# Clustered attention and token mixing on one core: a slot list for each half of the array's rows

## The chip, the cores and the metric

The kernel runs on one core of a Trainium2 chip. The metric is the device time of one execution in microseconds (us); lower is better. Five engines work side by side on a core: TensorE (PE, with its weight loads PEld), VectorE (DVE), ScalarE (ACT), GpSimd (POOL) and SyncE (SP), whose queue issues nearly all DMAs here. Each engine has a queue of its own, and in the profile an instruction that waits holds up what stands behind it on its engine.

## The reference

```python
# q, k, v: 4 batches x 8 heads x 768 x 64; centroids: 8 x 16 x 64
q_assign = np.argmax(np.einsum('bhsd,hcd->bhsc', q_n, c_n), axis=-1)    # normalised q, centroids
k_assign = np.argmax(np.einsum('bhsd,hcd->bhsc', k_n, c_n), axis=-1)
mask = q_assign[:, :, :, None] == k_assign[:, :, None, :]
scores = np.where(mask, scale * np.matmul(q, k.transpose(0, 1, 3, 2)), -1000000000.0)
attn = np.exp(scores - np.max(scores, axis=-1, keepdims=True))
attn = attn / (np.sum(attn, axis=-1, keepdims=True) + 1e-09)
x = (attn @ v), heads side by side                                       # 4 x 768 x 512
theta = x @ w_theta
y = w_tok_r @ (x * cos(theta)) + w_tok_i @ (x * sin(theta))              # over the 768 tokens
u = x + y
out = u + np.maximum(u @ w_ch, 0.0)
```

## The kernel before

**Stages.** Attention comes first (about 25 to 437 us of the profiled execution), token mixing second (from there to the end); the first rotation of the second stage is already computed while attention ends.

**Attention.** Two heads form a *pair* (16 pairs, `pi`). The two heads lie in the two halves of the 128 partitions, `j` = 0 in rows 0 to 63 and `j` = 1 in rows 64 to 127, so a matmul of one head uses half of the array's rows, and two matmuls with different `j` run side by side. Here such a place for one matmul of each half is called a **slot**. A *unit* is one tile of 128 keys for one half of the queries (12 units to a pair, 192 in all). For each unit and head the scores take four matmuls into one PSUM bank (`score_products`, tile `sc`), an exponential on ACT (`exps`, L437, tile `at`), a running sum over three tiles on POOL (`add_exps`, L448, tile `acc`), and two matmuls of the weighted sum (`weighted`, L509, tile `av`). The row maxima that the scores need are computed ten units ahead: four matmuls per head into two banks (`max_products`, tile `m`), reduced by one DVE instruction (`max_of`, L396).

**A block.** The main loop (L702) takes two units, `u` and `u + 1`, in a pass, which is called a **block** here; six blocks make a pair. A block has 12 slots and eight matmuls of weighted sums, in this order: four slots with both heads of unit `u` (`both`), four with head 0 of `u + 1` beside the maxima of one head of unit `u + 10` (`scores_beside_max`), the weighted sums of the two units before, and four slots with head 1 of `u + 1` beside the maxima of the other head. Blocks are named below by their first unit within the pair: 0, 2, 4, 6, 8, 10.

**Banks.** PSUM has eight: four for two `m` tiles, one for `av`, three that rotate (`bank`, L199), used for the scores and for all small results (`lg`, `lt`, `mt`, `rt`, `sm`). A rotating pool hands out the bank that was handed out longest ago, and the first matmul into it waits until its last reader is done.

**Pieces.** Everything else in attention is cut into small pieces that are given out by a table of due units: `pieces(u)` runs those due up to `u`, ahead of the weighted sums, behind them, and at the end of the block. On PE: `mt` (the transposed maxima, L404), `lg` and `lt` (the cluster products and their transposes, L263, L275), `sm` (sums, L476). On DVE: the argmax over 16 clusters, which reads `lt` in PSUM (L278 the maximum, L280 where it is reached, L284 and L286 its index), `mk` (L339), `add_sums` (L452), and the unpacking of weights (L137, L140, L143, L146). On POOL: the low parts `lq`, `lk` (L360), `xt` times `rb` (L530), the low parts of weights (L159). On ACT: copies out of PSUM, the high parts (L356), the mask's `Abs` and `Relu` (L335, L337). Within attention the code's order is the order on every engine (`in_order`). After it, the framework's scheduler orders the instructions.

**The end of attention.** `first_rotation` (L550) loads 128 tokens twice: `xs` for the angle `theta` (L608), and `xb`, four DMAs (L596) that DVE turns into token-major `xn` (L601). There is one `xb` buffer, so the DMAs of the next block wait for the turn before. DVE reduces the angle with L613, L614, L615; the bank of the next angle's matmuls is free once L614 has read it.

Of the kernel before, what the change touches and what calls it, by code (L numbers as in the profile page):

```python
# [9 lines left out]
F32 = mybir.dt.float32  # L10
# [6 lines left out]
PSUM = bass.MemoryType.PSUM  # L17

BIG = float(2.0 ** 60)
N_M = 2  # L20
N_AV = 1
# [20 lines left out]
def kernel(  # L42
# [136 lines left out]
    actx = ExitStack()  # L179

    ps0 = actx.enter_context(tc.tile_pool(name="ps0", bufs=N_M, space=PSUM))
    ps = actx.enter_context(tc.tile_pool(name="ps", bufs=8 - 2 * N_M - N_AV, space=PSUM))
# [13 lines left out]
    def m_tile(name):  # L196
        return ps0.tile([P, 2, 512], F32, tag="m", name=name)

    def bank(name):  # L199
        return ps.tile([P, 512], F32, tag="bank", name=name)  # L200
# [47 lines left out]
    def assign(pi):  # L248
# [172 lines left out]
    def score_products(u, j, banks=None):  # L421
# [5 lines left out]
        sc = banks[:, j] if banks else ps.tile([P, 512], F32, tag="bank", name=f"sc{u}_{j}")  # L427
# [28 lines left out]
        for j in range(2):  # L456
            then(u, j)

    def scores_beside_max(u, v, j):

        interleave(score_products(u, j), max_products(v, 1 - j))
        exps(u, j)
        max_of(v, 1 - j)

    def sums(pi):

# [47 lines left out]
                s["xt"] = p2.tile([P, 2, HS], F32, tag="xt", name=f"xt{pi}", bufs=3)  # L514

    def weighted_out(u):
        pi, a, i = split_u(u)
        s = st[pi]
        if i == NT - 1:

            if u == NUT - 1:
# [28 lines left out]
    def first_rotation():  # L550

        xs = ma[0].tile([P, NCT, P], F32, tag="ab", name="xs")
        nc.sync.dma_start(out=xs, in_=xT_d[0][:, :, 0:P])
        yield
        load_blocks(0)
# [4 lines left out]
        rotation_turn(0, xn)  # L560
        yield
        rotation_angle(xh, xl, tp)
        yield
        ab = rotation_reduce(0, "0_0", tp, kk, r)
        first.update(r=r, ab=ab, xn=xn)

    first = {}
# [134 lines left out]
    while u <= NUT or todo:  # L702
        start = len(nc.cur_bb.bb.instructions)
        ahead = u + LEAD

        def pieces(u):
            for x in sorted(x for x in todo if x <= u):
                for fn, a in todo.pop(x):
                    fn(*a)

        if 0 <= u < NUT:
            both(score_products, u, exps)
            add_exps(u)
            if ahead < NUT:
                scores_beside_max(u + 1, ahead, 0)
# [12 lines left out]
        if 0 <= u < NUT:  # L728
            if ahead < NUT:
                scores_beside_max(u + 1, ahead, 1)  # L730
            else:

                both(score_products, u + 1, exps, *([m_tile(f"sc{u + 1}")] if u < NUT - 6 else []))
            add_exps(u + 1)
        if 0 < u and ahead < NUT:
            weighted_out(u - 1)
        pieces(u + 1)
        in_order(start)
        u += 2
# [64 lines left out]
    def theta(b, t):  # L804
        n, name = b * NT + t, f"{b}_{t}"
        xs = xts[b][:, :, t * P:(t + 1) * P]
        xh, xl, xn, kk, r = rotation_tiles(n, name)

        late = n == AHEAD
        rotation_parts(xs, xh, xl, last_out[0] if late else None)  # L810
        rotation_turn(n, xn)
        tp = mbank(f"tp{name}")
        with behind(last_rows[0] if late else None):
            rotation_angle(xh, xl, tp)
        ab = rotation_reduce(n, name, tp, kk, r)
        rotate(b, t, r, ab, xn)

    def rotate(b, t, r, ab, xn):
# [188 lines left out]
```

## Time and profile before

| | |
|---|---|
| times of three runs | 795.07, 795.83, 797.3 us (median 795.83) |
| profiled execution | 797.01 us, of which the profile's span is 795.2 us |
| PE, DVE, ACT, POOL busy | 97%, 72%, 49%, 61% of the span |
| attention's steady part | 60 to 420 us of the span |
| one block without pieces on PE | 3.88 us |
| one pair (six blocks with their pieces) | 25.95 us |

The page gives shares over the whole span; attention and token mixing have quite different limits, so the views by stretches of time, and the timeline of single engines, tell more. In a timeline row the first number is the start in us from the span's start, the second the time until the group's last instruction ended, then engine, line, operation, what it writes and reads, and the count; the bracket holds idle time of the engine ahead of it and what ended it. A matmul of 384 columns stands with 0.33 to 0.34 us though the next begins 0.17 us behind it: ends overlap, so starts are compared.

### The profile page before, as it was taken

The numbers are of one execution on the slowest core, as the hardware profiler recorded it, in microseconds if no ns is written. First come the engines' busy times: TensorE is split into PE (matmuls) and PEld (weight loads), VectorE is DVE, ScalarE is ACT, GpSimd is POOL, SyncE is SP. The second block draws the span as 40 slices with busy tenths as digits, with TensorE's granted clock in tenths as the row PEclk, the third lists the DMA queues.
The fourth block names the chain that finished last, engine by engine and source line by source line (L and its number), as shares of the span: only waits on it lengthen the run. The fifth ranks groups of instructions, "written<-read, shape, count | busy, mean of one in ns | idle before, by whom it ended". The sixth has DMA issues, their size and how long they took to land.

```text
span 795.2 us, 14306 instructions
## 1 busy us (share of the span) xinstructions
PE 774.7 (97%) x5538; PEld 574.3 (72%) x5538; DVE 573.3 (72%) x688; ACT 386.9 (49%) x777; POOL 488.4 (61%) x284
## 2 busy tenths in 40 slices
PE   7999999999999999999999599999999999999998
PEld 5665656565665666666665378899888988899998
DVE  5889999999999999999889368954435343634322
ACT  3466666666767676666655335451324123403310
POOL 3479888999999999888988141571125122332131
PEclk9999999999999999999999899999999999999999
DMA  3233314342443234433352267024111411030001
GB/s 120 61 96 97 110 55 148 124 115 73 143 132 112 85 127 152 131 108 125 123 187 69 68 177 237 17 41 166 20 27 28 158 28 27 14 93 14 1 21 61
DMA packets 81584, 73.45 MB, mean 92 GB/s; under 512 B 59588, under 2 KB 65324, under 8 KB 81132
## 3 DMA queue, kind: packets, MB, share of 16 engines
q1 hardware_dynamic: 81228, 72.10, 30.5%
q8 instruction: 44, 0.72, 0.4%
q10 hardware_dynamic: 288, 0.43, 0.1%
q14 instruction: 24, 0.20, 0.1%
HBM read 57.08 MB, written 15.32 MB: 91 GB/s over the span
## 4 chain that ended last, share of the span: by engine, by line
PE 92%; DVE 5%; DMA 1%; SPq 1%; issue 1%; ACT 1%; DVEq 0%; ACTq 0%
PE y L876 26%; PE sc L374 25%; PE av L509 16%; PE tp L608 8%; PE cy L899 5%; PE m L374 3%; PE cp L899 3%; PE sm L476 2%; PE lg L263 1%; PE y L899 1%; DVE nm L396 1%; PE lt L275 1%; PE mt L404 1%; DVE acc L452 1%; SPq L596 1%
## 5 line engine op out<-in xcount | busy, mean ns | idle before, releaser
L437 ACT ACTIVATE at<-sc 128x384 f32<-128x384 f32 x384 | 173.6, 494 | 96.7 <-PE m L374 57.7
L396 DVE TENSOR_REDUCE nm<-m 128x1 f32<-128x768 f32 x192 | 179.7, 945 | 19.6 <-PE m L374 16.6
L448 POOL TENSOR_TENSOR acc<-at,at 128x768 f32<-128x768 f32 x64 | 130.4, 2038 | 40.0 <-ACT at L437 40.0
L374 PE MATMUL m<-hk,hq 64*128 64x384 f32 x384 | 147.2, 388 | 0.9 <-DVE nm L396 0.8
L509 PE MATMUL av<-at,vt 128*64 128x384 f32 x768 | 145.7, 499 | 1.4 <-ACT at L437 1.1
L448 POOL TENSOR_TENSOR acc<-acc,at 128x768 f32<-128x768 f32 x64 | 131.7, 2059 | 10.1 <-ACT at L437 8.0
L830 POOL TENSOR_TENSOR zlc<-ab,zhc 128x512 fp32r<-128x512 f32 x24 | 32.1, 1336 | 172.1 <-ACT zhc L828 172.1
L374 PE MATMUL m<-mk,mq 64*128 64x384 f32 x384 | 127.7, 336 | 0.6 <-DVE mk L303 0.6
L374 PE MATMUL sc<-hq,hk 64*128 64x384 f32 x384 | 117.0, 389 | 0.5 <-ACT at L437 0.5
L374 PEld LDWEIGHTS sc<-hq,hk 64*128 64x128 f32 x384 | 55.8, 183 | 61.9 <-issue 27.8
L374 PE MATMUL sc<-lq,hk 64*128 64x384 f32 x384 | 97.6, 335 | 0.0
L374 PE MATMUL sc<-mq,mk 64*128 64x384 f32 x384 | 97.4, 334 | 0.0
L374 PE MATMUL sc<-hq,lk 64*128 64x384 f32 x384 | 97.2, 333 | 0.0
L509 PEld LDWEIGHTS av<-at,vt 128*64 128x64 f32 x768 | 46.7, 136 | 60.5 <-issue 53.6
L613 DVE TENSOR_SCALAR kk<-tp 128x512 int32<-128x512 f32 x24 | 16.4, 683 | 79.4 <-PE tp L608 79.4
L374 PEld LDWEIGHTS m<-hk,hq 64*128 64x128 f32 x384 | 70.6, 185 | 3.5 <-DVE nm L396 2.7
L374 PEld LDWEIGHTS m<-mk,mq 64*128 64x128 f32 x384 | 71.3, 187 | 1.0 <-ACT hq L356 1.0
L452 DVE TENSOR_TENSOR acc<-acc,acc 128x768 f32<-128x768 f32 x30 | 70.7, 2357 | 0.0
L581 ACT CAST xh<-xT 128x512 fp32r<-128x512 f32 x23 | 14.3, 622 | 99.8 <-PE tp L608 99.8
L890 POOL TENSOR_TENSOR ul<-xT,uh 128x384 fp32r<-128x384 f32 (+1 forms) x36 | 33.5, 955 | 35.5 <-ACT uh L889 34.9
L374 PEld LDWEIGHTS sc<-lq,hk 64*128 64x128 f32 x384 | 54.9, 185 | 0.0
L374 PEld LDWEIGHTS sc<-mq,mk 64*128 64x128 f32 x384 | 54.9, 184 | 0.0
(160 smaller groups left out, 1713.3 us busy)
## 6 DMA issues: line engine op xcount, KB each, us to landing
rawq<-in_qT_dram SPq DMA_DIRECT2D x16, 384.0 KB
vt<-in_v_dram SPq DMA_DIRECT2D x16, 384.0 KB
rb<-sd SPq DMA_DIRECT2D x32, 192.0 KB
xT_d<-xt SPq DMA_DIRECT2D x16, 384.0 KB
xb<-xT_d SPq DMA_DIRECT2D x96, 64.0 KB
rawk<-in_kT_dram SPq DMA_DIRECT2D x15, 384.0 KB
w<-in_wrT_dram SPq DMA_DIRECT2D x6, 768.0 KB
w<-in_wiT_dram SPq DMA_DIRECT2D x6, 768.0 KB
```

Of the source, the lines that this page charges most:

```text
L374: nc.tensor.matmul(out, lhsT=stat[r, cols], rhs=mov[r, over], start=start, stop=stop)
L396: nc.vector.tensor_reduce(out=s["nm", a][:, j, i // 2:i // 2 + 1], in_=s["m", j][:, :, 0:HS], op=ALU.max, axis=AX.XY, negate=True)
L437: last_exp[0] = nc.scalar.activation(out=s["at", a, i][:, j], in_=s["sc", j], func=AF.Exp, scale=SCALE)
L448: last_acc[0] = nc.gpsimd.tensor_tensor(out=s["acc", a, x], in0=prev, in1=at, op=ALU.add)
L452: nc.vector.tensor_tensor(out=s["acc", a, 0], in0=s["acc", a, 0], in1=s["acc", a, 1], op=ALU.add)
L509: nc.tensor.matmul(s["av"][64 * j:64 * j + 64], lhsT=s["vt"][:, i, j, :], rhs=s["at", a, i][:, j], start=(i == 0), stop=(i == NT - 1))
L608: nc.tensor.matmul(tp, lhsT=xx[:, c, :], rhs=w_th[c][k], start=(n == 0), stop=(n == 3 * NCT - 1))
L613: nc.vector.tensor_scalar_mul(kk, tp, INV_2PI)
L830: nc.gpsimd.tensor_tensor(out=zl, in0=tr, in1=zh.bitcast(F32), op=ALU.subtract)
L876: nc.tensor.matmul(y_at(b, d, c0, c1), lhsT=zz[:, d * P:(d + 1) * P], rhs=ww[:, c0:c1], start=first and lead, stop=last, skip_group_check= ...
L890: nc.gpsimd.tensor_tensor(out=ul[:, d, :], in0=x, in1=uh[:, d, :].bitcast(F32), op=ALU.subtract)
L899: nc.tensor.matmul(cp, lhsT=w_c[d][k][:, e * P:(e + 1) * P], rhs=uu[:, d, :], start=(n == 0), stop=(n == 3 * NCT - 1), skip_group_check=True)
```

## The change

Four things are edited.

1. **Slots.** `scores_beside_max` is replaced by `two_units(u, v)`, which writes all 12 slots of a block. Each half has a list of its own, and the groups of four matmuls of half 1 begin three slots behind those of half 0. The last score matmul of half 1 is carried into slot 0 of the next block. Slots with maxima hold `max_of` at their ends (slots 8 and 11), and the copy of a finished weighted sum comes in slot 3 of a later block. Each of the three banks gets a tag of its own and is handed out by a planned time at which it is free (`clock`, `free_at`).
2. **Pieces.** In blocks with maxima all pieces due up to `u` come ahead of the weighted sums; those due at `u + 1` stay behind them.
3. **Argmax.** From pair 2 on `lt` lies in a rotating bank and not in an `m` tile; ACT copies it into SBUF (`lts`), and L278 and L280 read the copy.
4. **Turns.** `rotation_turn` comes behind `rotation_reduce`, and the first `xb` load comes right behind that of `xs`.

```diff
+    clock = [0.0]
+    free_at = [0.0] * NB
+    SLOTS, AV_SLOTS, EXP_SLOTS = 12, 8, 5
+
+    def bank(name, until=None):
+        x = min(range(NB), key=lambda i: (free_at[i], i))
+        free_at[x] = until if until is not None else clock[0] + AV_SLOTS
+        return ps.tile([P, 512], F32, tag=f"bank{x}", name=name)
...
-        lt = (m_tile(f"lt{pi}")[:, 0] if pi > 1 else bank(f"lt{pi}"))[:, 0:HS]
+        lt = bank(f"lt{pi}")[:, 0:HS]
...
+        if pi > 1:
+            lts = pe.tile([P, HS], F32, tag="lgs", name=f"lts{pi}")
+            nc.scalar.copy(out=lts, in_=lt)
+            lt = lts
...
-    def scores_beside_max(u, v, j):
-
-        interleave(score_products(u, j), max_products(v, 1 - j))
-        exps(u, j)
-        max_of(v, 1 - j)
...
+    def two_units(u, v):
...
+        rows = {(1, 0): carry[0]} if carry else {}
+        first = [(exps, u - 1, 1), (add_exps, u - 1)] if carry else []
...
+        begin = {
+            0: (scores, u, 0, 0, 1, 2, 3), 1: (maxima, 1, 1, 2, 7, 8), 3: (scores, u, 1, 3, 4, 5, 6),
+            4: (maxima, 0, 4, 5, 10, 11), 6: (scores, u + 1, 0, 6, 7, 8, 9), 9: (scores, u + 1, 1, 9, 10, 11)}
+        end = {
+            0: first, 3: [(exps, u, 0), (weighted_out, u - 3)], 6: [(exps, u, 1), (add_exps, u)],
+            8: [(max_of, v, 1)], 9: [(exps, u + 1, 0)], 11: [(max_of, v, 0)]}
+        for k in range(SLOTS):
+            clock[0] = t0 + k
+            if k in begin:
+                fn, *a = begin[k]
+                fn(*a, **(dict(more=1 + AV_SLOTS) if k == 9 else {}))
+            interleave(*([rows[j, k]] for j in range(2) if (j, k) in rows))
+            for fn, *a in end.get(k, ()):
+                fn(*a)
...
-        pieces(u - 0.5)
+        pieces(u if ahead < NUT else u - 0.5)
...
-        rotation_turn(n, xn)
         tp = mbank(f"tp{name}")
         with behind(last_rows[0] if late else None):
             rotation_angle(xh, xl, tp)
         ab = rotation_reduce(n, name, tp, kk, r)
+        rotation_turn(n, xn)
```

**PE, inside a block.** Before, units 68 and 69 (`sc68_0` is head 0 of unit 68, `m78_1` the maxima of head 1 of unit 78):

```order
L374 MATMUL sc68_0_2431<-hq_2_152,lk_2_155 128x384
L374 MATMUL sc68_1_2432<-hq_2_152,lk_2_155 128x384
L374 MATMUL sc68_0_2431<-mq_2_156,mk_2_157 128x384
L374 MATMUL sc68_1_2432<-mq_2_156,mk_2_157 128x384
L374 MATMUL sc69_0_2445<-hq_2_152,hk_2_154 128x384
L374 MATMUL m78_1_2447<-hk_0_163,hq_0_161 128x384
L374 MATMUL sc69_0_2445<-lq_2_153,hk_2_154 128x384
L374 MATMUL m78_1_2447<-mk_0_166,mq_0_165 128x384
```

The same units after the change, slots 5 to 8:

```order
L386 MATMUL m78_0_2455<-mk_0_166,mq_0_165 128x384
L386 MATMUL sc68_1_2450<-hq_2_152,lk_2_155 128x384
L386 MATMUL sc69_0_2461<-hq_2_152,hk_2_154 128x384
L386 MATMUL sc68_1_2450<-mq_2_156,mk_2_157 128x384
L386 MATMUL sc69_0_2461<-lq_2_153,hk_2_154 128x384
L386 MATMUL m78_1_2445<-hk_0_163,hq_0_161 128x384
L386 MATMUL sc69_0_2461<-hq_2_152,lk_2_155 128x384
L386 MATMUL m78_1_2445<-mk_0_166,mq_0_165 128x384
```

Before, both halves ended their groups in the same slot and the next slot began two groups at once; now half 0 begins `sc69_0` in a slot in which half 1 is at the last matmul of `sc68_1`, and only one group begins in a slot.

**DVE, from block 10 to block 2 of a pair.** `m_0` and `m_1` are the two tiles of maxima (L396, after the change L408); the rows begin with the argmax. Before:

```order
L278 TENSOR_REDUCE mxl_2892<-lt_2888 128x24
L280 TENSOR_TENSOR eq_2894<-lt_2888,mxl_2892 128x384
L396 TENSOR_REDUCE nm_2800<-m_0_2897 128x1
L284 TENSOR_TENSOR eq_2894<-eq_2894,wc 128x384
L286 TENSOR_REDUCE rr_2910<-eq_2894 128x24
L396 TENSOR_REDUCE nm_2800<-m_1_2927 128x1
L396 TENSOR_REDUCE nm_2800<-m_0_2945 128x1
L452 TENSOR_TENSOR acc_2778<-acc_2778,acc_2866 128x768
L396 TENSOR_REDUCE nm_2977<-m_1_2978 128x1
L137 TENSOR_SCALAR w_2837<-w_2837 128x768
L396 TENSOR_REDUCE nm_2977<-m_0_3009 128x1
L140 TENSOR_SCALAR w_2837<-w_2837 128x768
```

And after (the same instructions, whose lines in the changed code are L290, L292, L408, L296, L298, L464, L137 and L140):

```order
L290 TENSOR_REDUCE mxl_2914<-lts_2912 128x24
L292 TENSOR_TENSOR eq_2916<-lts_2912,mxl_2914 128x384
L296 TENSOR_TENSOR eq_2916<-eq_2916,wc 128x384
L298 TENSOR_REDUCE rr_2923<-eq_2916 128x24
L408 TENSOR_REDUCE nm_2800<-m_1_2931 128x1
L408 TENSOR_REDUCE nm_2800<-m_0_2940 128x1
L464 TENSOR_TENSOR acc_2798<-acc_2798,acc_2889 128x768
L408 TENSOR_REDUCE nm_2979<-m_1_2980 128x1
L408 TENSOR_REDUCE nm_2979<-m_0_2990 128x1
L137 TENSOR_SCALAR w_2856<-w_2856 128x768
L140 TENSOR_SCALAR w_2856<-w_2856 128x768
```

The two reductions of a block now stand together and the pieces of a block stand together behind them: no reduction lies any more between L292 and L296, nor between L137 and L140.

**DVE, at the end of attention.** `xn_0` and `xn_1` are the turned blocks of the first two rotations, `sq` the last but one pair's sums, `kk_0`, `r_0` the reduction of the first angle. Before:

```order
L146 SCALAR_TENSOR_TENSOR w_5615<-w_5614,w_5615 128x768
L601 STREAM_TRANSPOSE xn_0_5829<-xb_5822 128x512
L601 STREAM_TRANSPOSE xn_1_6062<-xb_5846 128x512
L494 RECIPROCAL sq_5886<-sq_5886 128x12
L613 TENSOR_SCALAR kk_0_5830<-tp_0_5844 128x512
L614 SCALAR_TENSOR_TENSOR r_0_5831<-kk_0_5830,tp_0_5844 128x512
L615 SCALAR_TENSOR_TENSOR r_0_5831<-kk_0_5830,r_0_5831 128x512
```

After:

```order
L146 SCALAR_TENSOR_TENSOR w_5648<-w_5647,w_5648 128x768
L546 RECIPROCAL sq_5908<-sq_5908 128x12
L667 TENSOR_SCALAR kk_0_5858<-tp_0_5872 128x512
L668 SCALAR_TENSOR_TENSOR r_0_5859<-kk_0_5858,tp_0_5872 128x512
L669 SCALAR_TENSOR_TENSOR r_0_5859<-kk_0_5858,r_0_5859 128x512
L655 STREAM_TRANSPOSE xn_0_5857<-xb_5783 128x512
```

Both turns moved behind the reduction that they stood ahead of (`xn_1` behind that of the second angle). On the SP queue the loads of the second `xb` move with them: before, they stood ahead of the store `wd5i` (L156), the load of `sq` (L492) and its store (L495); now behind all three.

More of the change, by code (lines that the diff above doesn't have):

```diff
@@ L426, in score_products @@
             s["at", a, i] = p3.tile([P, 2, HS], F32, tag="at", name=f"at{u}", bufs=NAT)
-        sc = banks[:, j] if banks else ps.tile([P, 512], F32, tag="bank", name=f"sc{u}_{j}")
+        sc = banks[:, j] if banks else bank(f"sc{u}_{j}", until)
         sc = s["sc", j] = sc[:, 0:HS]
@@ L457, in both, with finish, scores, maxima @@
             then(u, j)
-    def scores_beside_max(u, v, j):
-        interleave(score_products(u, j), max_products(v, 1 - j))
-        exps(u, j)
-        max_of(v, 1 - j)
+    carry = []
+    def finish(u):
+        while carry:
+            interleave(carry)
+            carry.clear()
+            exps(u, 1)
+            add_exps(u)
+    def two_units(u, v):
+        rows = {(1, 0): carry[0]} if carry else {}
+        first = [(exps, u - 1, 1), (add_exps, u - 1)] if carry else []
+        carry.clear()
+        t0 = clock[0]
+        def scores(u, j, *slots, more=0):
+            last = slots[-1] + more
+            for slot, x in zip((*slots, SLOTS), score_products(u, j, until=t0 + last + 1 + EXP_SLOTS)):
+                if slot < SLOTS:
+                    rows[j, slot] = x
+                else:
+                    carry.append(x)
+        def maxima(j, *slots):
+            for slot, x in zip(slots, max_products(v, j)):
+                rows[j, slot] = x
+        begin = {
[12 more added lines that the diff above has]
+                fn(*a)
+        clock[0] = t0 + SLOTS
     def sums(pi):
@@ L727 @@
         pieces(u)
[L728 to L733, printed above, removed]
+        if 0 <= u < NUT and ahead >= NUT:
+            both(score_products, u + 1, exps, *([m_tile(f"sc{u + 1}")] if u < NUT - 6 else []))
             add_exps(u + 1)
-        if 0 < u and ahead < NUT:
-            weighted_out(u - 1)
         pieces(u + 1)
```

25 lines of the change are left out of this document (15 added, 10 removed).

## The prediction

> **What bounds the kernel now.** I read the page's busy shares, then the busy times by stretches of time, then the timelines of single engines.
>
> ```profile
> PE 774.7 (97%) x5538; PEld 574.3 (72%) x5538; DVE 573.3 (72%) x688; ACT 386.9 (49%) x777; POOL 488.4 (61%) x284
> ```
>
> ```profile
> 100.00:200.00 100.00, 99.57 (x820) 60.81 (x818) 96.95 (x93) 65.56 (x141) 93.75 (x47) 1.00 0.35 103
> 200.00:300.00 100.00, 100.00 (x826) 61.08 (x824) 94.69 (x94) 68.73 (x146) 97.79 (x47) 1.00 0.36 118
> 300.00:400.00 100.00, 100.00 (x824) 61.24 (x822) 93.46 (x91) 64.17 (x137) 90.65 (x43) 1.00 0.42 132
> ```
>
> Over the span PE leads by far. In the steady part of attention (columns: PE, PEld, DVE, ACT, POOL, clock) three engines are nearly full: PE 100%, DVE 93 to 97%, POOL 91 to 98%. So a block that PE does faster needs DVE and POOL to follow.
>
> PE's 100% hides gaps, since ends overlap. In one block without pieces:
>
> ```profile
> 200.31 1.51 PE L509 MATMUL av<-at,vt 128*64 128x384 f32 x8
> ...
> 202.56 0.34 PE L374 MATMUL sc<-hq,hk 64*128 64x384 f32 x2
> ...
> 202.73 0.33 PE L374 MATMUL sc<-lq,hk 64*128 64x384 f32 x2
> ...
> 202.75 0.49 ACT L437 ACTIVATE at<-sc 128x384 f32<-128x384 f32 x1 [0.95 <-PE m L374]
> ...
> 203.08 0.34 PE L374 MATMUL sc<-mq,mk 64*128 64x384 f32 x2
> ...
> 203.29 0.18 PEld L374 LDWEIGHTS sc<-hq,hk 64*128 64x128 f32 x1 [0.20 <-ACT at L437]
> 203.30 0.44 PE L374 MATMUL sc<-hq,hk 64*128 64x384 f32 x1
> ...
> 203.58 0.34 PE L374 MATMUL sc<-lq,hk 64*128 64x384 f32 x1
> ...
> 204.19 1.51 PE L509 MATMUL av<-at,vt 128*64 128x384 f32 x8
> ...
> 205.63 0.27 PE L404 MATMUL mt<-identf,nm 128*6 128x128 f32 x1
> ...
> 206.62 0.44 PE L374 MATMUL sc<-hq,hk 64*128 64x384 f32 x1
> ```
>
> A slot takes 0.17 us (202.56 to 202.73) but 0.22 ahead of 203.30 and 0.28 behind it: that group's bank is held by the exponential that ran from 202.75 to 203.24, and after the wait the weights load uncovered. The loss is 0.05 + 0.11, about 0.15 us of the 3.88 us from one `av` to the next.
>
> **Slots: what they remove.** Now five slots, not four, lie between the last matmul into a bank and the first of the next group in it. With 0.28 us for a block's first slot and 0.175 for the others, slot 3 begins at 0.63 us and its matmul ends at 0.97; ACT starts 0.04 later, takes 0.49, and the bank is free at 1.55; slot 9 needs it at 1.68. Slot 6 needs its bank at 1.16 and gets it at 1.03. ACT has 1.7 us for other work between a block's last exponential and the carried one, and its longest other lines take 0.8 to 0.9 us, two of them in blocks 0 and 6. So I cost the bank waits at zero afterwards: 91 blocks x 0.15 = **13.7 us** at most, 0.9 a pair. Moved ahead of `av`, the small matmuls change only places; I give that nothing.
>
> **What they cost on DVE.** Before, the maxima of a block ended in slots 3 and 11, so DVE's two reductions came 1.4 and 2.5 us apart, and each `m` tile was free again some 1.8 us before its next use. Now they are ready 0.52 us apart, 1.88 and 2.40 us after a block begins, and their tiles are needed again 0.28 and 0.81 us into the next. At 0.87 us each, DVE may be late by 0.8 us (with pieces on PE 1.2) before PE waits. And the pieces between them now stand together. What that does follows from DVE and POOL:
>
> ```profile
> 216.88 2.31 DVE L452 TENSOR_TENSOR acc<-acc,acc 128x768 f32<-128x768 f32 x1
> 219.11 0.94 DVE L396 TENSOR_REDUCE nm<-m 128x1 f32<-128x768 f32 x1
> 219.97 1.33 DVE L137 TENSOR_SCALAR w<-w 128x768 f32<-128x768 f32 x1
> 221.22 0.94 DVE L396 TENSOR_REDUCE nm<-m 128x1 f32<-128x768 f32 x1
> 222.09 1.31 DVE L140 TENSOR_SCALAR w<-w 128x768 int32<-128x768 int32 x1
> ...
> 224.19 1.71 DVE L143 SCALAR_TENSOR_TENSOR w<-w,w 128x768 int32<-128x768 int32 x1
> ...
> 227.56 0.94 DVE L146 SCALAR_TENSOR_TENSOR w<-w,w 128x768 int32<-128x768 int32 x1
> ```
>
> ```profile
> 220.85 2.14 POOL L448 TENSOR_TENSOR acc<-acc,at 128x768 f32<-128x768 f32 x1
> 222.94 2.15 POOL L360 TENSOR_TENSOR lq<-rawq,hq 128x768 fp32r<-128x768 f32 x1
> ```
>
> L137 ends at 221.30, 0.45 us behind the start of a POOL instruction; L140 at 223.40, 0.46 behind the next. Both seem to wait until POOL's instruction ends and then need 0.45 us; the reductions from PSUM do not wait (0.94 each). Two such instructions in a row pay a whole POOL instruction, as this L140, right behind an L137:
>
> ```profile
> 426.19 2.07 DVE L140 TENSOR_SCALAR w<-w 128x768 int32<-128x768 int32 x1
> ```
>
> So L140, now right behind L137, goes from 1.24 (with its overlap) to 2.07 us. The argmax:
>
> ```profile
> L280 DVE TENSOR_TENSOR eq<-lt,mxl x16: 557/558/559, 11.5 to 367.4; 128x384 bf16<-128x384 f32 x16
> ```
>
> ```profile
> L284 DVE TENSOR_TENSOR eq<-eq,wc x16: 357/1498/1672, 12.1 to 368.8; 128x384 bf16<-128x384 bf16 x16
> ```
>
> L280 reads `lt` from PSUM and takes 0.558 us every time; L284 has the same 384 elements, both inputs in SBUF, and takes 0.36 to 1.67. With `lts` both inputs of L280 lie in SBUF. Bounds: 0.56 (never waits) to 0.56 + 1.5; I take 1.45, by L284. L284, now directly behind it, costs between 0.36 and 2.07; I take 2.0, by L140. The Trainium skill, page "GPSIMD Engine Reference", section "Specifications", says the same of the cause: POOL's SBUF interfaces are shared with DVE, which contends when it has two SBUF inputs or runs in a 2-port mode. By that rule the copy makes L280 a contender, which the L284 row agrees with.
>
> The other pieces:
>
> ```profile
> 205.21 1.23 DVE L339 TENSOR_SCALAR mk<-clk,mcl,mbi 128x768 fp32r<-128x768 f32 x1
> 206.36 2.59 DVE L452 TENSOR_TENSOR acc<-acc,acc 128x768 f32<-128x768 f32 x1
> ...
> 231.16 1.25 DVE L339 TENSOR_SCALAR mk<-clk,mcl,mbi 128x768 fp32r<-128x768 f32 x1
> ```
>
> Per block, in us: block 8 has `mk` 1.15, L452 2.5 and a reciprocal 0.15, together 3.8; block 10 the two reductions of the argmax at about 0.55 each, 1.45 and 2.0, together 4.5; block 0 L452 2.25; block 2 L137 1.25 and L140 2.07, 3.3; block 4 L143 1.65; block 6 L146 0.95. A pair now lasts 25.95 us (231.16 - 205.21). Without bank waits PE's blocks last 3.75 us and their small matmuls (1.0 for `mt` and `lg` in block 8, 205.63 to 206.62; 0.5, 0, 0.35, 0.75 and 0 in the others, read in the same way): 4.8, 4.25, 3.75, 4.1, 4.5, 3.75, a pair 25.1.
>
> Now add up, from the start of block 8 with DVE on time. Its reductions are done at 3.6 and its pieces at 7.4. Block 10 starts at 4.8 and its first maxima are ready at 6.7: DVE is 0.8 late, done with them at 9.2 and with the pieces at 13.7. Block 0 starts at 9.0, its maxima are ready at 10.9: 2.8 late, and the tiles come free at 14.5 and 15.4. Block 2 starts at 12.75 and needs them at 13.0 and 13.6: **PE waits** 1.5, and 0.3 more at slot 4. L452 and then L137, L140 make DVE 2.0 late again in block 4, and block 6 waits 0.35. Blocks 4 and 6 are light and end the lag. What is queued behind the waiting matmul is everything on PE, so ACT's exponentials and POOL's sums wait with it. Together 2.2 us of waits against 0.9 gained: a pair **1.3 us longer**. With the lower values (L280 0.9, L284 1.5, L140 1.25) the waits are 0.4 and a pair is 0.5 us shorter. As a pair grows, POOL has more idle time and DVE waits for it less (POOL's 12 instructions a pair don't grow); I take 0.8 us longer: 14 pairs x 0.8 = **+11**, and the blocks of the first and last pair, without the argmax, **-1**.
>
> The copy `lts` on ACT costs 0.48 us in block 10 under ACT's idle time (64 to 69% busy); if that cover went, slot 6 would be late.
>
> **Turns: what they remove.**
>
> ```profile
> 432.92 2.57 DVE L146 SCALAR_TENSOR_TENSOR w<-w,w 128x768 int32<-128x768 int32 x1
> ...
> 440.84 0.71 DVE L601 STREAM_TRANSPOSE xn<-xb 128x512 f32<-128x512 f32 x1 [4.73 <-DMA xb<-xT_d]
> 442.13 0.23 DVE L494 RECIPROCAL sq<-sq 128x12 f32<-128x12 f32 x1 [0.58 <-DMA sq<-sd]
> ...
> 442.94 0.69 DVE L614 SCALAR_TENSOR_TENSOR r<-kk,tp 128x512 f32<-128x512 int32 x1
> ```
>
> ```profile
> 439.46 0.43 SPq L492 DMA_DIRECT2D sq<-sd  x1
> ```
>
> ```profile
> 434.20 1.19 PE L608 MATMUL tp<-wth_hi,xh 128*128 128x512 f32 x4
> ...
> 437.97 0.34 PE L374 MATMUL sc<-hq,hk 64*128 64x384 f32 x1
> 443.77 2.04 PE L608 MATMUL tp<-wth_hi,xh 128*128 128x512 f32 x4 [5.47 <-DVE r L614]
> ...
> 449.05 0.44 PE L374 MATMUL sc<-hq,hk 64*128 64x384 f32 x1
> ```
>
> PE stands for 5.5 us until L614, which stands behind the second turn and its late DMA. With the turns behind the reductions the reciprocal is late next: `sq` is loaded behind the store `wd5i`, which waits for L146 (435.5); so it issues at 436.2, lands 2.65 later (as from 439.46 to 442.1), L614 ends at 440.4 and PE goes on at 440.5, **3.3 us** earlier. The second block's loads, moved behind three DMAs, are needed only by L825, behind both angles' reductions. Then the clock:
>
> ```profile
> 440.00:460.00 20.00, 12.62 (x60) 6.96 (x61) 10.17 (x13) 6.66 (x11) 5.36 (x3) 0.81 0.33 93
> ```
>
> The granted clock falls to 0.81 here: the 12 matmuls from 443.77 last 5.3 us, four of them 2.04 against 1.19 at 434.20, so about 3.0 at full clock. If 2.2 us of idle PE no longer bring that on, 2.3 more are gained; between nothing and 2.3 I take the middle, 1.2, since 2.2 us of idle PE lie between none and the 5.5 of this row. Sum: **-4.5 us**. The Trainium skill, page "TensorE: Matmul & The Clock Gate", section "What's actually happening", has the clock halved after an idle window of about 3.4 us, free-running; by that rule the whole 2.3 is gained, and the change would be worth -5.6 here.
>
> Against the profiled execution's own 797.0 (span 795.2 and 1.8 around it): 797.0 + 11 - 1 - 4.5 = 802.5. That execution lies 1.2 over the median of the runs, so I say **802 us**.
>
> **Rivals.**
> - *DVE and POOL follow* (the other side): the pieces find POOL idle, lags stay under 0.8 to 1.2 us, and all or most of 0.9 a pair stays. For it: DVE idles 3 to 7%, L146 above took 0.94 without any wait. Against: DVE's additions are about 2.2 us a pair, more than its idle time of 0.8 to 1.7. It decides where the two argmax instructions take under 2.4 us together. From -5 to -13.7, with the turns 778 to 788; middle 783. Chance 0.22.
> - *A draw in attention*: waits on DVE eat just what the slots gain, only the turns count: 797 - 4.5, about 792 (-3 to +2 around it). Chance 0.22, of which half lies within 0.3%.
> - *Full price*: every DVE piece pays as worked out or more, 14 x 1.3 and up: 811 to 818. Chance 0.12.
> - *The change does not do what it says*: ACT is late and the stall moves to slots 6 and 9; no gain, less pressure on DVE: 793 to 797. Chance 0.04.
> - The forecast, 796 to 810: 0.40.
>
> **How the numbers follow.** 0.3% (2.4 us) is about what a measurement can tell from no change, so 793.4 to 798.2 is the same. Faster: 0.22 + half of the draw 0.11 + 0.01 = 0.34. Same: 0.11 + 0.03 + 0.02 from the lower edge of the forecast = 0.16. Slower: 0.38 + 0.12 = 0.50. The range takes in the forecast, the draw, half of each outer rival: 783 to 815; the forecast's own is 796 to 810.
>
> **What would show it.** Right: slots 7 and 8 of a block at 0.175 us; waits of PE on DVE's L408 at slots 1 and 4, most in blocks 2 and 6; L292 near 1.4 and L296 and L140 near 2 us; DVE 97% or more busy; PE's gap behind the first rotation near 2.2 us. Wrong: L292 still at 0.56 us, no waits of PE on DVE, a steady pair of 25.1 us; or waits of PE on ACT, which I cost at zero.

## The result, and the profile after

The changed kernel is **slower by 1.6%**: 809.62 us (median of four runs, 806.0 to 811.04) against 795.79 us in the runs of before made beside it; ratio 1.016, interval 1.0133 to 1.0187. The sign is that of the forecast and the time lies in its range, but +6 us were forecast and +13.8 measured. The profiled execution after took 808.54 us with a span of 806.5, 11.3 more than the 795.2 of before; it is these 11.3 that the views can divide.

The page of after, its busy shares and the chain that ended last by engine:

```profile
PE 774.3 (96%) x5538; PEld 574.6 (71%) x5538; DVE 580.0 (72%) x688; ACT 404.9 (50%) x791; POOL 486.1 (60%) x284
...
PE 68%; DVE 25%; ACT 3%; issue 2%; DMA 1%; SPq 0%; ACTq 0%; DVEq 0%
PE y L929 25%; DVE nm L408 10%; PE sc L386 9%; PE av L561 8%; PE tp L662 8%; PE m L386 6%; PE cy L952 5%; DVE acc L464 3%; PE cp L952 3%; DVE eq L296 2%; DVE eq L292 2%; DVE mk L351 2%; DVE w L143 2%; ACT at L449 1%; PE sm L528 1%
```

The same view of before:

```profile
PE 92%; DVE 5%; DMA 1%; SPq 1%; issue 1%; ACT 1%; DVEq 0%; ACTq 0%
```

Busy shares over the span hardly differ. The chain does: DVE held 5% of it and now holds 25%, with the reductions, both argmax instructions and the unpacking among its lines. The weighted sums stand once in a block and so divide the span: PE's timeline of before, at the first `av` of attention, the first of every sixth block after it, and the first `y` of token mixing (columns: start, time, engine, line, operation).

```profile
35.08 1.51 PE L509 MATMUL av<-at,vt 128*64 128x384 f32 x8
...
60.38 0.87 PE L509 MATMUL av<-at,vt 128*64 128x384 f32 x4
...
421.76 0.54 PE L509 MATMUL av<-at,vt 128*64 128x384 f32 x2 [0.24 <-ACT xt L524]
...
466.37 0.50 PE L876 MATMUL y<-wr_hi,zhc 128*128 128x512 f32 x2
```

The same places after, with one wait between the first two:

```profile
40.04 1.51 PE L561 MATMUL av<-at,vt 128*64 128x384 f32 x8
...
44.14 0.44 PE L386 MATMUL m<-hk,hq 64*128 64x384 f32 x1 [2.05 <-DVE nm L408]
...
67.65 0.54 PE L561 MATMUL av<-at,vt 128*64 128x384 f32 x2
...
438.87 1.51 PE L561 MATMUL av<-at,vt 128*64 128x384 f32 x8 [1.22 <-ACT xt L578]
...
477.64 0.50 PE L929 MATMUL y<-wr_hi,zhc 128*128 128x512 f32 x2
```

| stretch, in us | before | after | difference | in the forecast |
|---|---|---|---|---|
| start, to the first `av` | 35.1 | 40.0 | +5.0 | no term |
| first pair | 25.3 | 27.6 | +2.3 | -1 (with the last) |
| 14 pairs | 361.4 | 371.2 | +9.8 | +11 |
| from there to the first `y` | 44.6 | 38.8 | -5.8 | -4.5 |
| token mixing | 328.9 | 328.9 | 0 | 0 |

The steady part by stretches (columns: PE, PEld, DVE, ACT, POOL, clock):

```profile
100.00:200.00 100.00, 96.81 (x804) 60.20 (x802) 95.54 (x92) 71.06 (x144) 93.23 (x46) 1.00 0.36 116
200.00:300.00 100.00, 95.80 (x785) 58.25 (x783) 96.99 (x84) 68.46 (x139) 92.45 (x45) 1.00 0.35 109
300.00:400.00 100.00, 97.54 (x803) 59.94 (x801) 96.32 (x94) 68.98 (x140) 87.94 (x42) 1.00 0.39 124
```

PE fell from 100 to 96 to 98%, so now it waits; DVE stands at 96 to 97%. What PE waits for, from 60 to 460 us (columns: in total, times, longest). The first row is that of the weight loads, the second that of the matmuls behind them; they tell mostly of the same waits and are not to be added:

```profile
PEld m L386 <- DVE nm L408: 18.6, 30, 1.8
...
PE m L386 <- DVE nm L408: 8.0, 11, 1.5
```

In blocks without such a wait the slots do what was forecast. Slots 6 to 9 of one:

```profile
202.09 0.34 PE L386 MATMUL sc<-hq,hk 64*128 64x384 f32 x1
...
202.26 0.33 PE L386 MATMUL sc<-lq,hk 64*128 64x384 f32 x1
...
202.44 0.34 PE L386 MATMUL m<-mk,mq 64*128 64x384 f32 x1
...
202.62 0.34 PE L386 MATMUL sc<-mq,mk 64*128 64x384 f32 x1
```

They begin 0.17 to 0.18 us apart, also where half 0 begins a new bank (slot 6), without the 0.05 and 0.11 that the bank's wait took before. The wait of 2.05 us at 44.14 shows what took their place. DVE ahead of it:

```profile
38.05 0.55 DVE L290 TENSOR_REDUCE mxl<-lts 128x24 f32<-128x384 f32 x1 [0.52 <-ACT lts L286]
38.64 2.10 DVE L292 TENSOR_TENSOR eq<-lts,mxl 128x384 bf16<-128x384 f32 x1
40.78 1.86 DVE L296 TENSOR_TENSOR eq<-eq,wc 128x384 bf16<-128x384 bf16 x1
42.67 0.55 DVE L298 TENSOR_REDUCE rr<-eq 128x24 f32<-128x384 bf16 x1
43.14 1.81 DVE L408 TENSOR_REDUCE nm<-m 128x1 f32<-128x768 f32 x2
```

and POOL beside it:

```profile
38.50 1.83 POOL L460 TENSOR_TENSOR acc<-at,at 128x768 f32<-128x768 f32 x1 [6.78 <-ACT at L449]
40.41 2.02 POOL L460 TENSOR_TENSOR acc<-acc,at 128x768 f32<-128x768 f32 x1
```

L292 began 0.14 us behind the start of a POOL instruction and ended 0.41 behind its end; L296 the same with the next (0.21 behind 42.43). The two took 3.96 us where 0.92 is what they need, the two reductions began only at 43.14, and PE, which needed their first tile at 42.1, went on at 44.14. The two reductions of the argmax, 0.55 each, did not wait. Pair by pair the same shows: two full pairs in which both instructions ran undisturbed (0.56 and 0.36) took 25.34 and 25.32 us; the nine in which one or both met a POOL instruction took 26.39 to 28.43; one more undisturbed pair took 26.18. DVE itself had no long wait for a result of POOL from 60 to 440 us: 15.6 us of its waits there are for PE's maxima and 1.6 for ACT. Over the whole run:

```profile
L296 DVE TENSOR_TENSOR eq<-eq,wc x16: 357/1864/1936, 12.0 to 383.8; 128x384 bf16<-128x384 bf16 x16
...
L292 DVE TENSOR_TENSOR eq<-lts,mxl x14: 557/797/2152, 38.6 to 383.2; 128x384 bf16<-128x384 f32 x14
```

```profile
L140 DVE TENSOR_SCALAR w<-w 128x768 int32<-128x768 int32 (+1 forms) x16 | 31.2, 1950 | 0.6
...
L296 DVE TENSOR_TENSOR eq<-eq,wc 128x384 bf16<-128x384 bf16 x16 | 19.4, 1214 | 0.6
...
L292 DVE TENSOR_TENSOR eq<-lts,mxl 128x384 bf16<-128x384 f32 x14 | 15.6, 1113 | 0.5
```

### The profile page after: what moved, and what is told of

Its sections match the earlier page's. It is cut to its first block, busy times and chain, and to the rows that moved or that the text cites. A ratio compares the mean times of both kernels' runs of the same rounds, so it can differ in the third digit from the quotient of the medians.

```text
span 806.5 us, 14280 instructions
## 1 busy us (share of the span) xinstructions
PE 774.3 (96%) x5538; PEld 574.6 (71%) x5538; DVE 580.0 (72%) x688; ACT 404.9 (50%) x791; POOL 486.1 (60%) x284
## 4 chain that ended last, share of the span: by engine, by line
PE 68%; DVE 25%; ACT 3%; issue 2%; DMA 1%; SPq 0%; ACTq 0%; DVEq 0%
PE y L929 25%; DVE nm L408 10%; PE sc L386 9%; PE av L561 8%; PE tp L662 8%; PE m L386 6%; PE cy L952 5%; DVE acc L464 3%; PE cp L952 3%; DVE eq L296 2%; DVE eq L292 2%; DVE mk L351 2%; DVE w L143 2%; ACT at L449 1%; PE sm L528 1%
## 5 line engine op out<-in xcount | busy, mean ns | idle before, releaser
L449 ACT ACTIVATE at<-sc 128x384 f32<-128x384 f32 x384 | 185.4, 494 | 115.9 <-PE sc L386 102.7
L408 DVE TENSOR_REDUCE nm<-m 128x1 f32<-128x768 f32 x192 | 173.5, 943 | 25.5 <-PE m L386 25.2
L460 POOL TENSOR_TENSOR acc<-at,at 128x768 f32<-128x768 f32 x64 | 136.6, 2134 | 29.2 <-ACT at L449 29.1
L386 PE MATMUL m<-hk,hq 64*128 64x384 f32 x384 | 133.3, 352 | 12.1 <-DVE nm L408 10.8
L386 PE MATMUL sc<-hq,hk 64*128 64x384 f32 x384 | 137.1, 367 | 2.2 <-ACT at L449 1.0
L386 PE MATMUL sc<-mq,mk 64*128 64x384 f32 x384 | 134.8, 359 | 0.0
L386 PE MATMUL sc<-lq,hk 64*128 64x384 f32 x384 | 127.2, 339 | 0.0
L386 PE MATMUL sc<-hq,lk 64*128 64x384 f32 x384 | 126.5, 337 | 0.0
L386 PEld LDWEIGHTS sc<-hq,hk 64*128 64x128 f32 x384 | 68.8, 184 | 62.4 <-issue 28.5
L386 PEld LDWEIGHTS sc<-lq,hk 64*128 64x128 f32 x384 | 69.5, 185 | 0.0
L386 PEld LDWEIGHTS sc<-mq,mk 64*128 64x128 f32 x384 | 69.0, 184 | 0.6 <-issue 0.6
L386 PEld LDWEIGHTS sc<-hq,lk 64*128 64x128 f32 x384 | 69.1, 184 | 0.0
```

Source lines behind the costliest of these rows:

```text
L386: nc.tensor.matmul(out, lhsT=stat[r, cols], rhs=mov[r, over], start=start, stop=stop)
L408: nc.vector.tensor_reduce(out=s["nm", a][:, j, i // 2:i // 2 + 1], in_=s["m", j][:, :, 0:HS], op=ALU.max, axis=AX.XY, negate=True)
L449: last_exp[0] = nc.scalar.activation(out=s["at", a, i][:, j], in_=s["sc", j], func=AF.Exp, scale=SCALE)
L460: last_acc[0] = nc.gpsimd.tensor_tensor(out=s["acc", a, x], in0=prev, in1=at, op=ALU.add)
```

## The experiments

The theory: in attention DVE is late, because its instructions with SBUF inputs wait for whole POOL instructions and now stand together, and PE waits for its tiles; the turns gain at the end; at the start something else is lost, perhaps the banks. All runs stand here; the stretches are read from the same rows as above, and the ratios are to runs of before on the same chip. The ratio and the difference of the medians are up to some 2 us apart, so an effect is sure only to about that.

| run | median us | ratio, interval | first `av` | first pair | mean of 14 pairs | to first `y` |
|---|---|---|---|---|---|---|
| before | 795.79 | | 35.1 | 25.3 | 25.81 | 44.6 |
| after | 809.62 | 1.016 (1.0133 to 1.0187) | 40.0 | 27.6 | 26.52 | 38.8 |
| t1_turns | 791.09 | 0.9934 (0.9915 to 0.9952) | 35.1 | 25.3 | 25.81 | 39.0 |
| t2_start | 803.16 | 1.0105 (1.0068 to 1.0142) | 35.9 | 27.6 | 26.26 | 38.8 |
| t3_no_unpack | 798.95 | 1.003 (1.0015 to 1.0046) | 41.8 | 27.6 | 25.81 | 37.8 |
| t4_no_copy | 801.24 | 1.0066 (1.0043 to 1.0089) | 40.5 | 27.1 | 26.00 | 37.8 |
| u1_pool_half | 790.32 | 0.993 (0.9903 to 0.9958) | 39.9 | 29.1 | 25.19 | 37.9 |
| u2_spread | 829.53 | 1.0399 (1.0355 to 1.0443) | 36.7 | 27.1 | 28.34 | 37.9 |
| u3_no_adds | 802.06 | 1.0065 (1.0043 to 1.0088) | 37.1 | 30.0 | 26.04 | 39.7 |
| u4_pieces_back | 820.52 | 1.0308 (1.0273 to 1.0343) | 41.2 | 31.7 | 27.14 | 37.9 |
| v1_start_no_copy | 797.43 | 0.9997 (0.9973 to 1.0022) | 38.2 | 27.1 | 25.90 | 37.8 |
| v2_sums_early | 847.1 | 1.0611 (1.0576 to 1.0645) | 38.3 | 27.1 | 29.34 | 37.9 |
| v3_sums_early_copy | 847.0 | 1.0609 (1.0589 to 1.0628) | 35.9 | 30.0 | 29.42 | 37.8 |
| w1_mk_early | 809.53 | 1.0194 (1.0143 to 1.0245) | 37.6 | 28.0 | 26.54 | 37.9 |

### The turns alone (t1_turns)

The kernel before, with the fourth edit only:

```diff
-        rotation_turn(n, xn)
         tp = mbank(f"tp{name}")
...
         ab = rotation_reduce(n, name, tp, kk, r)
+        rotation_turn(n, xn)
```

> The kernel before with the turns alone (the fourth edit). Theory: PE waits less behind the first rotation, and the stretch from the last weighted sum of attention to the first token mixing matmul (44.6 us before, 38.7 us after the whole change) falls by 4.5 to 6 us: about 790 us, 788 to 792. Rival, that this stretch fell because of the new slots at the end of attention and not by the turns: 794 to 796 us, and the clock falls to half twice as before.

A ratio of 0.9934, some 5 us less than before. Attention is the same to 0.1 us, and only the last stretch is shorter, by 5.65. PE at its two angles:

```profile
434.07 1.20 PE L608 MATMUL tp<-wth_hi,xh 128*128 128x512 f32 x4
...
439.52 1.17 PE L608 MATMUL tp<-wth_hi,xh 128*128 128x512 f32 x4 [1.36 <-DVE r L614]
```

The second begins 4.25 us earlier than the 443.77 of before, waits 1.36 us and not 5.47, and runs at full clock: 1.17 us for four, against 2.04. Of the kernels that compute the whole result this is the only one that is faster than the kernel before.

### The start (t2_start)

```diff
-    clock = [0.0]
+    clock = [-1.0]
+    given = [0]
...
-        x = min(range(NB), key=lambda i: (free_at[i], i))
+        x = min(range(NB), key=lambda i: (free_at[i], i)) if clock[0] >= 0 else given[0] % NB
+        given[0] += 1
```

> The changed kernel, but its three banks are given out in turn until the first block with scores. Theory: the changed kernel's planner gives every small result at units below 0 the same bank (the one whose planned time stays lowest), and that makes the start late: first weighted sum at 35 to 36 us in place of 40.0, and 803 to 805 us against 809.6. Rival, that the pieces' order or the moved loads make the start late: first weighted sum still near 40 us, 808 to 811 us.

In the change `clock` is 0 until the loop and -100 at its first unit (-10), so a bank that is given out there is planned free at -92, ahead of the 8 of the others, and is taken again for each small result, which then waits for its last reader. PE of the changed kernel at the start:

```profile
13.44 0.51 PE L310 MATMUL ot<-identb,clq 128*128 128x128 bf16 x6 [0.22 <-DVE clq L303]
14.84 0.49 PE L310 MATMUL ot<-identb,clq 128*128 128x128 bf16 x6 [0.89 <-ACT mq L313]
...
33.84 0.44 PE L386 MATMUL sc<-hq,hk 64*128 64x384 f32 x1 [0.66 <-ACT lgs L275]
```

With banks in turn the wait for `mq` is gone and the first `av` stands at 35.88:

```profile
12.68 0.84 PE L312 MATMUL ot<-identb,clq 128*128 128x128 bf16 x12 [0.19 <-DVE clq L305]
...
35.88 0.54 PE L563 MATMUL av<-at,vt 128*64 128x384 f32 x2
```

Like is to be set beside like here, with the copy or without it. With the copy the four kernels with the change's planner have the first `av` at 39.9 to 41.8 (mean 40.7) and the three with banks in turn at 35.9 to 37.1 (36.3); without it the one with the planner has 40.5 and the four in turn 36.7 to 38.3 (37.7); these five wait 1.2 us for L292's bank ahead of it. The two kernels with the old start have 35.1. So in the change the banks are 4.4 us of the start's loss; about 1 us stays open. The first pair did not move (27.6): its loss is another.

### Less DVE work (t3_no_unpack)

```diff
+        late = new is not raw_pair
+        if late:
+            nc.vector.tensor_scalar(
...
         yield
+        if late:
...
```

> The changed kernel without three of the four DVE instructions that unpack each early weight (L137, L140, L143 left out; the weights are then wrong, the copies and stores stay). About 5.3 us of DVE work a pair goes. Theory, that a steady pair is long because DVE is late with the maxima: PE's waits on L408 nearly vanish and a steady pair falls from 26.5 us (mean) to 25.1 to 25.5: 790 to 797 us. Rival, that ACT or the banks set the pair: pairs stay above 26.2, 806 to 810 us.

Half of it came. The pair falls by 0.71 us, to 25.81, not to 25.5 or less, and the waits halve:

```profile
PEld m L390 <- DVE nm L412: 9.1, 16, 1.2
...
PE m L390 <- DVE nm L412: 3.6, 7, 0.9
```

What is left of PE's waits stands at slot 1 of block 2, behind the argmax and L464, which this run keeps. So DVE's work is part of what sets the pair; the rival, with pairs above 26.2, did not hold.

### No copy (t4_no_copy)

```diff
-        if pi > 1:
+        if pi > NPAIR:
             lts = pe.tile([P, HS], F32, tag="lgs", name=f"lts{pi}")
```

> The changed kernel without the copy: the argmax reads its bank in PSUM. Theory, that two SBUF inputs make L292 wait for POOL: L292 falls from 1.11 to 0.56 us each, DVE has 0.5 us less a pair, and where the bank is not missed the time falls by 2 to 6 us: 804 to 808. Rival, that the copy costs nothing on DVE: L292 stays near 1.1 us. If the bank is held too long by the late DVE, PE waits for DVE's L292 at a score group and the time rises instead, to 811 to 816.

```profile
L292 DVE TENSOR_TENSOR eq<-lt,mxl x16: 557/558/559, 11.4 to 376.0; 128x384 bf16<-128x384 f32 x16
L296 DVE TENSOR_TENSOR eq<-eq,wc x16: 357/774/1952, 12.0 to 376.6; 128x384 bf16<-128x384 bf16 x16
```

```profile
PE sc L386 <- DVE eq L292: 5.1, 9, 0.8
...
PEld m L386 <- DVE nm L408: 2.5, 9, 0.4
```

L292 is 0.558 us every time again, although POOL is as busy. The waits on L408 fall from 18.6 to 2.5; 5.1 us of waits for L292's bank take their place, nine times at most 0.8. Net 0.52 us a pair, and the ratio to before falls by 0.0094 from that of the change, 7.5 us: more than I gave it. In the first pair the wait of 2.05 us is gone, but the pair falls only from 27.6 to 27.1: DVE reaches L137 and L140 earlier, they now meet POOL there (1.86 and 2.03 us, in the change 0.42 and 0.43), and PE waits for L408 in the next two blocks instead (0.54 and 0.22 us, and the weight loads uncovered behind them).

### Less POOL work (u1_pool_half)

```diff
-        if y > 0:
+        if y == 1:
             prev = s["at", a, i - 1] if y == 1 else s["acc", a, x]
```

> The changed kernel with half of POOL's additions left out (every third unit's exponentials are not added, so the sums are too small); nothing of DVE's or PE's program changes. Theory, that DVE is late because its instructions on SBUF wait for POOL: L292 falls from 1.11 to 0.6 to 0.8 us, L140 from 1.95 to under 1.3, PE's waits on L408 vanish, a steady pair is 25.1 to 25.5 us: 790 to 797 us. Rival, that the amount of DVE's own work or its new order makes it late, whatever POOL does: L292 and L140 within 10% of before, pairs above 26.2: 806 to 810 us.

This decides between the two readings of "DVE is late": DVE's program is the same, and only its neighbour does less.

```profile
L296 DVE TENSOR_TENSOR eq<-eq,wc x16: 357/359/1861, 11.9 to 368.0; 128x384 bf16<-128x384 bf16 x16
...
L292 DVE TENSOR_TENSOR eq<-lts,mxl x14: 557/558/2107, 38.5 to 367.5; 128x384 bf16<-128x384 f32 x14
```

```profile
PEld m L386 <- DVE nm L408: 1.2, 3, 0.4
```

L292 and L296 are at 0.56 and 0.36 us nearly always, PE's waits on L408 are gone, and a pair takes 25.19 us, near what the forecast had for a pair without waits (25.1; the full pairs here take 25.25 to 25.8, and the mean holds two shorter ones). L140, right behind L137, stays at 1.77 us (mean of 16) where under 1.3 was expected: where two such instructions follow each other the second still waits.

### The other edits of the attention part (u4_pieces_back, u3_no_adds)

The second edit undone:

```diff
-        pieces(u if ahead < NUT else u - 0.5)
+        pieces(u - 0.5)
```

> The changed kernel with the second edit undone (the pieces due at a block's first unit stand behind its weighted sums again). Theory, that the second edit only moves places: 806 to 810 us; the transposed maxima (0.33 us each in the changed kernel, 0.25 before) wait less for DVE, worth 1 to 2 us at most. Rival, that the pieces in front of the weighted sums are what costs in attention: 800 us or less.

Neither: the ratio rises from 1.016 to 1.0308, some 12 us **more**. In the profiled executions the first pair is 4.0 us longer than in the change and each of the 14 others 0.63. ACT's copy and so the argmax come behind the weighted sums' 1.5 us; DVE stands 7.0 us in all for the copy (11 times, from 60 to 460 us; in the change it has no such wait there), and L292 then meets POOL for most of an instruction more often than not:

```profile
L292 DVE TENSOR_TENSOR eq<-lts,mxl x14: 874/2167/2174, 40.0 to 396.8; 128x384 bf16<-128x384 f32 x14
```

L292 takes 0.65 us more in the mean (1.77 for 1.11) and L296 0.29 less, so the two alone are not the whole loss; how the rest divides is not shown. So, beside the other edits, the second is worth some 12 us, and I had given it nothing.

Without L464, its sum made on PE (and banks in turn):

```diff
-        nx = NT // TERMS if pi == NPAIR - 1 else 1
+        nx = NT // TERMS
...
-        if pi < NPAIR - 1:
-            for a in range(2):
-                at_unit(7 if pi == a == 0 else u + ADDS[a], add_sums, pi, a)
```

> The changed kernel with banks in turn at the start, and without L464: PE adds the two halves of each sum itself (four more matmuls a pair). DVE loses 3.6 us a pair. Theory: PE's waits on L408 (1.1 us a pair) vanish and 0.4 to 0.8 us of matmuls a pair come in their place, also in the first pair: against the 803.2 of the start alone 4 to 10 less, 793 to 799. Rival, that the argmax's two instructions make the lag alone: the wait in block 2 stays near 0.6 us a pair and the time is 801 to 806.

802.06: the rival's number, by another way. Of the 26.26 us of a pair with banks in turn 0.22 go: `sm` now takes 1.43 us of PE in place of 0.78 and eats most of what the waits give back. The first pair of 30.0 is in part a matter of the clock (see the last section).

### Moving DVE's pieces (v1_start_no_copy, u2_spread, v2_sums_early, v3_sums_early_copy, w1_mk_early)

First the two repairs together, with no piece moved.

> The changed kernel with banks in turn at the start and without the copy. The two effects measured apart were 6.5 and 8.4 us, of which the wait of the first pair (0.5 us less without the copy) and the clock at the start are counted in both. Theory, that they are two causes: 794 to 797 us. Rival, that they are one and the same (a late start): 800 to 803 us. It is also what the kernel with spread weights is to be set beside: if this one is near 795, moving the weights' steps alone cost 35 us.

Two causes: against the 1.016 of the change the ratio falls by 0.0055 with the banks, by 0.0094 without the copy and by 0.0163 with both. A pair takes 25.90 us, near the 25.81 of before, and the whole is level with before: the stretch to the first `y`, where the turns stand, is 6.8 us shorter and pays for what stays lost at the start (3.1), in the first pair (1.8) and in the 14 pairs (1.2). So the new slots do not pay here even with both repairs: the turns alone (t1_turns) are faster. Then three ways to spread the pieces:

```diff
-    W_UNITS = (8, 11.5, 14, 15, 16, 18, 19.5)
+    W_UNITS = (8, 11.5, 16, 17, 18, 19, 19.5)
```

> The changed kernel with three edits: banks in turn at the start, no copy (the argmax reads PSUM), and the weights' DVE steps moved to blocks 4, 4, 6, 6 (from 2, 2, 4, 6). If the effects of the first two add up (6.5 and 8.4 us by their runs, the wait of the first pair once), 795 us without the third. Theory, that lag comes from what stands together on DVE: no wait on L408 in blocks 2 and 6 is left and the third edit brings 1 to 4 more: 791 to 794 us. Rival, that it only moves the lag to blocks 6 and 8: 795 to 798 us.

```diff
-ADDS = (8, 13)
+ADDS = (6, 13)
```

> As the kernel with banks in turn and without the copy, and the first sum of a pair (L464, 2.1 us) moved from block 8 to block 6, so that block 8 of DVE is lighter ahead of the argmax. Theory, that the price of a DVE instruction is set by the lag that it meets: the waits for L292's bank in block 0 (0.5 us a pair) and for L408 in block 2 vanish, a steady pair falls from 26.0 to 25.3 to 25.6: 786 to 791 us. Rival, that it moves the lag to block 8, as the spread weights did: 797 us or more.

> The changed kernel with banks in turn and the first sum in block 6, and with the copy as in the change. Theory: block 10 begins 2 us less late on DVE, so that the argmax's 3 us with the copy make less lag: the wait in block 2 falls from 0.9 us a pair to 0.2 to 0.5, and against 803.2 the time is 4 to 10 us less: 793 to 799 us. Rival, that the argmax with the copy alone makes the lag: 801 to 804 us.

and `mk` moved ahead of the mask's first ACT step, with `W_FIRST` at (-4, -0.5, 4, 4, 5, 6, 7.5):

> As the kernel with banks in turn and without the copy, with DVE's mk (L351) moved from block 8 to block 6, whose inputs are there by then, and the first weight's steps two units later. Nothing is waited for that is not ready: mk reads only the broadcast rows, which the first ACT step of the mask reads at the same place. Theory (what counts is the lag at a block's start): block 8 of DVE is 1.2 us lighter, the argmax begins earlier, the wait for its bank in block 0 (0.5 us a pair) falls to 0.1 to 0.2, the first pair from 27.1 to 25.5 to 26.5: against 797.4 some 5 to 7 less, 790 to 793 us, so faster than before by 0.5%. Rival, that block 6's weights step and mk together (2.5 us) make a lag of their own in block 8: 796 to 802 us.

All four lost, by the medians 12 to 50 us against the kernels without the move (v1_start_no_copy, for v3 t2_start); beside v2's rival (797 us or more) none of the ranges named had it. One place of v2_sums_early, DVE, ACT and PE:

```profile
223.05 2.55 DVE L466 TENSOR_TENSOR acc<-acc,acc 128x768 f32<-128x768 f32 x1 [1.79 <-POOL acc L462]
225.53 2.55 DVE L146 SCALAR_TENSOR_TENSOR w<-w,w 128x768 int32<-128x768 int32 x1
```

```profile
228.11 0.83 ACT L158 CAST wr_hi<-w 128x768 fp32r<-128x768 f32 x1 [4.66 <-DVE w L146]
```

```profile
229.15 0.44 PE L388 MATMUL sc<-hq,hk 64*128 64x384 f32 x1 [3.35 <-ACT mr L429]
```

The sum (there L466) came before POOL's last addition was done; L146 stood behind it on DVE, ACT's copy of the weight behind L146, all of ACT's exponentials behind that copy, and PE behind them. In w1_mk_early the same copy waits up to 2.7 us for L146, now behind `mk`. For u2_spread the waits on L408 (18.5 us) and on the argmax's bank (11.1) show the lag moved and grown; why by 32 us is argued, not shown.

## Why the prediction was right and wrong

**The step that failed is the start.** The forecast's sum had three terms, attention's pairs, the turns and the first and last pair, and none for the blocks below unit 0, though the planner's times run from there and the case `clock = 0` to -100 could be read in the diff. It measured +5.0; t2_start, with 4.2 of these back, shows that the banks are most of it. The second miss is the term "the blocks of the first and last pair, without the argmax, -1": the first pair does have one, that of pair 2 (`A_THIRD` has units 0 and 1), and its L292 and L296, at 2.10 and 1.86 us, made the 2.05 us of wait at 44.14; without the copy that wait is gone, though the pair gets only 0.5 us shorter (t4_no_copy). With +5.0 and +2.3 in place of nothing and -1, the sum would have been about 810 by its own terms. (The forecast's 802.5, less the 1.2 that it names itself, is 801.3 and not 802; that changes nothing here.)

**Attention's middle was right** in sign, mechanism and place. That its size came out so near, +9.8 for +11, is in part luck, since its parts were both too large and balanced: without lag a pair takes 25.19 (u1_pool_half), so slots and pieces gain 0.62 us a pair, not 0.9 (the kernel before had 0.6 us of PE's waits on L396 in all its pairs, from 60 to 420 us); and the lag costs 26.52 - 25.19 = 1.33, not 1.7 (0.8 and the 0.9 gained). L140 came at 1.95 us (forecast 2.07); L292 at a mean of 1.11 (1.45) and L296 at 1.21 (2.0), since of 14 times both met a running POOL instruction in six, one of the two in four and neither in four. PE's waits stand in block 2, as named (9 of 11, at slot 1, 7.2 of 8.0 us); in block 6, named too, there is one of 0.4. "Moved ahead of `av`, the small matmuls change only places; I give that nothing" was wrong beside these edits: their place also sets when the argmax starts (u4_pieces_back).

**The turns**: -5.8 for -4.5, the mechanism right, its sizes not. I took 1.2 for the clock as the middle between nothing and 2.3. After the change:

```profile
451.70 1.20 PE L662 MATMUL tp<-wth_hi,xh 128*128 128x512 f32 x4
...
456.31 1.17 PE L662 MATMUL tp<-wth_hi,xh 128*128 128x512 f32 x4 [0.69 <-DVE r L668]
...
468.33 2.79 PE L528 MATMUL sm<-acc,ecol 128*32 128x384 f32 x16 [2.46 <-DVE xt L576]
```

and before:

```profile
458.00 1.76 PE L476 MATMUL sm<-acc,ecol 128*32 128x384 f32 x16 [2.46 <-DVE xt L522]
```

Both angles run at full clock (granted clock 1.00 from 440 to 460 us), so the whole 2.3 came, and the gap is 0.69 us, not 2.2: counted from the first `av` of the last pair, the second angle begins 4.6 us earlier, not 3.3. The rule weighed in the prediction, from the Trainium skill, page "TensorE: Matmul & The Clock Gate", section "What's actually happening", gave -5.6; for the two angles the trace agrees with it. That the sum comes so near is luck: the two gains make 6.9, and 1.1 is lost again behind them. The sums at 468.33 run at half speed (2.79 us against 1.76), in a stretch of the clock's record from 466.9 to 473.7 us that followed gaps of 1.31 and 2.46 us with 1.24 us of work between; PE never stood for 3.4 us on end there.

**The rivals.** "DVE and POOL follow" fell for this kernel, but in attention's steady part it would have held with half of POOL's additions left out (u1_pool_half). "ACT is late" fell too: no long wait of PE on an exponential, and t3_no_unpack and t4_no_copy shorten the pair without touching ACT's exponentials. What the runs show most plainly is the lock between DVE and POOL. The Trainium skill, page "SBUF — State Buffer", section "🔬 SBUF: two separate sides", says that a vector instruction with two SBUF inputs and a POOL instruction that reads SBUF exclude each other, and that the one that starts first keeps the shared ports to its end. The rows at 38.64 and 40.78 and the 0.558 us of t4_no_copy agree; PSUM as the source of one input takes the instruction out of it.

## What to carry to other kernels

A copy from PSUM to SBUF that frees a bank can make its reader compete with another engine: look at what each instruction of a nearly full engine shares before its operands are moved. Where three engines are over 90% full, a piece's place is worth more than its length, and each move has to be followed through every queue behind it. A planner with times of its own has to be read at its edges, the first units included, not only in the steady loop.

## What the runs showed of the hardware that was not expected

- The lock works both ways. DVE's sum of two SBUF tiles took 0.95 us where it began half a microsecond ahead of a POOL instruction (208.26 in v2_sums_early), and that one then 2.09 (208.82), against 1.83 undisturbed; begun 0.09 behind one it took 2.55 (223.05). The longest POOL additions after the change took 2.65.
- One and the same wait in the first pair, 2.03 to 2.06 us of PE on L408, is there in the change and six of its variants. In the change, t2_start and t3_no_unpack the clock stays at full speed behind it and the first pair takes 27.6 us. In u1_pool_half, u3_no_adds, u4_pieces_back and v3_sums_early_copy the trace's clock record has half speed for 3.4 us just there (45.8 to 49.2 in u1_pool_half). In u1_pool_half, where PE has no further wait on L408 in that pair, the first pair takes 29.1 us, 1.5 more; the other three have further waits of 0.5 to 0.8 us in it and take 30.0 to 31.7. Why the clock fell in four of the seven was not tried.
- The first `av` lies at 35.9 to 37.1 us in the three kernels with banks in turn and the copy. How much of the start runs at half speed does not decide it: before has 3.4 us of that ahead of its first `av` and t1_turns 10.2, and both stand at 35.1; u2_spread has 10.2 and stands at 36.7, v1_start_no_copy 6.8 and 38.2. Whether it matters where the half-speed stretches fall was not tried.
